# Attention with 192 queries and 1,024 keys: the third key load put behind a blank slot in one piece, and the output stores moved two pairs later

## The chip, the cores and the metric

The kernel runs on one core of one Trainium2 chip. The metric is the device time in microseconds (us). The profile is of one further execution; its span, from the first to the last instruction, was 812.8 us, in a run whose device time was 814.49 us.

## The reference

For 16 x 32 = 512 heads, with 192 queries, 1,024 keys and a head size of 128, all in bf16:

```python
B, H, Sq, Sk, D = 16, 32, 192, 1024, 128
...
scores = jnp.einsum("bhqd,bhkd->bhqk", q, k) * scale
p = _softmax(scores, axis=-1)
return jnp.einsum("bhqk,bhkd->bhqd", p, v)
```

## The kernel before

**Tiling.** Four heads make a *quad*; there are NQ = 128 quads, numbered x. The scores of one quad are made in three *fills* of PSUM, so there are NF = 384 fills, numbered f, and fill f belongs to quad f // 3. Each fill has a matching step of the second product, numbered s, which runs LAG = 4 fills later. TensorE's program is a plain alternation: `qk(f)` (L655, its matmuls at L670), then `pv(f - LAG)` (L678, matmuls at L699). One fill with its step takes about 2.05 us of TensorE, and one quad three times that. Ahead of fill 0 there is one blank fill (PRE = 1) and six blank steps (BLANK = 6) on cleared data, so that the loop's first round is like all others. The loop on TensorE (L715) holds six fills; what comes after it is straight code.

**The other engines.** VectorE transposes K (`turn_k`, L763, three pieces to a quad, three fills ahead) and Q (`turn_q`, L772), and normalises each finished step (`onorm`, L784 and L788) into the output buffer `f_ob`. GpSimd copies K into the order that TensorE reads (`order`, L620) and spreads V beside columns of ones (`spread`, L629). ScalarE takes the exponentials (L861, L864). There is one accumulator `f_o`, so `pv(s)` waits on `s_on` until `onorm(s - 1)` has read it. VectorE works strictly in its written order: while it waits for a K load, the `onorm` behind that transposition waits too, and TensorE with it.

**Loads.** K and V have five slots each (1 MB to a quad, 192 KB more for Q). All but one of the loads are issued by SyncE (SP) in one fixed order on one queue: each next V, then K, then Q, each held until its slot is free (`load_k` waits on `s_kx`, `load_v` on `s_pv`). At the start the order is written out by hand (L573 to L586). There, SP waits for two things: `s_qk >= PRE + 1` (fill 0 has been computed), and `s_pv >= BLANK - 2` (four of the blank steps are done). The load of quad 2's K stands around that second wait, in two halves of 512 KB.

**Stores.** The outputs of two quads (a *pair*) make one store of 384 KB; the last two quads are stored singly, the very last one in two halves. Slot i % NSO of `f_ob` holds store i. ScalarE issues store i after fill 6i + 12 + 6 * HOLD, which is seven pairs after the fills of that pair (`store_at`, L539). What would fall into the last 12 fills is left to SP, which issues it behind its last load (L596). With HOLD = 7 these are stores 54 to 64.

**The end.** After the last step VectorE checks the reciprocals, TensorE sums the two flags (L729, L730), all engines meet, each reads a flag that decides whether a general path has to be run (it isn't for this data), and SP waits in `stored` (L601) until every store has landed.

Of the kernel before, what the change touches and what calls it, by code (L numbers as in the profile page):

```python
# [421 lines left out]
def _attention_kernel(nc, q, k, v, out):  # L422
# [9 lines left out]
    NF = 3 * NQ  # L432
    LAG = 4

    PRE = 1
# [3 lines left out]
    NKN, NVS, NKT, NVP = 5, 5, 2, 2  # L439
    GQ = 2  # L440

    NSO, HOLD = 10, 7

    HELD = 2
    VB = 136
# [9 lines left out]
    with ExitStack() as outer:  # L455
        redo = outer.enter_context(nc.sbuf_tensor("redo", [1, 1], mybir.dt.int32))

        def sem(name):
            return outer.enter_context(nc.semaphore(name))
# [5 lines left out]
        s_kn = [sem("f_kn%d" % i) for i in range(NKN)]  # L465
# [7 lines left out]
        s_qk = sem("f_qk")  # L473
# [11 lines left out]
        with ExitStack() as es:  # L485
# [34 lines left out]
            def store(e, i):  # L520
                so = i % NSO
                x, c = stores[i]
                if x + c == NQ:

                    for y in range(2):
                        e.wait_ge(s_fin, y + 1)
                        e.dma_start(
                            of[4 * x + 2 * y:4 * x + 2 * y + 2].rearrange("x (p j) d -> (x p) (j d)", j=3),
                            ob[:, so, 3 * y:3 * y + 3, :].rearrange("p j d -> p (j d)"),
                        ).then_inc(s_st[so], 16)  # L530
                    return
                e.wait_ge(s_rc, 3 * (x + c) + 1)
                e.dma_start(
                    of[4 * x:4 * x + 4 * c].rearrange("(a x) (p j) d -> (x p) a (j d)", x=2, j=3),
                    ob[:, so, 0:6 * c, :].rearrange("p (a j) d -> p a (j d)", j=3),
                ).then_inc(s_st[so], 16)


            store_at = {3 * (x + c) + 6 + 6 * HOLD: i for i, (x, c) in enumerate(stores)  # L539
                        if 3 * (x + c) + 6 + 6 * HOLD <= NF - 12}  # L540

            def load_q(e, x):
                e.dma_start(
                    qn[:, x % NKN, :],
                    qf[4 * x:4 * x + 4].rearrange("a (j u) d -> (a j) (u d)", u=6).bitcast(U32),
                ).then_inc(s_qn[x % NKN], 16)
# [3 lines left out]
            def hint(eng):  # L550
                hints[eng.engine] = eng.mark_branch_hint_location()

            @block.sync
            def _(e):
                def load_k(x, lo=0, hi=32):
                    if x >= NKN:
                        e.wait_ge(s_kx, 3 * (x - NKN) + 3)
                    e.dma_start(
                        kn[:, x % NKN, 64 * lo:64 * hi],
                        kf[4 * x:4 * x + 4].rearrange("a (j r) d -> (a j) r d", r=32)[:, lo:hi, :]  # L560
                        .rearrange("p r d -> p (r d)").bitcast(U32),
                    ).then_inc(s_kn[x % NKN], 16)

                def load_v(x, lo=0, hi=4):
                    if x >= NVS:
                        e.wait_ge(s_pv, 3 * (x - NVS) + 2 + BLANK)
                    e.dma_start(
                        vs[:, x % NVS, lo:hi, :],
                        vf[4 * x + lo:4 * x + hi].rearrange("a (m t) d -> m a (t d)", t=T),
                    ).then_inc(s_v[x % NVS], 16)  # L570


                load_k(0)  # L573
                e.wait_ge(s_blank, 1)
                load_k(1)
                load_q(e, 1)
                load_v(0, 0, 2)
                e.wait_ge(s_qk, PRE + 1)
                load_v(0, 2, 4)
                load_k(2, 0, 16)  # L580
                e.wait_ge(s_pv, BLANK - 2)
                load_k(2, 16, 32)
                load_q(e, 2)
                for n in range(3, NKN):
                    load_v(n - 2)
                    load_k(n)  # L586
                    load_q(e, n)
                for n in range(NQ):
                    if n == NQ // 2:
                        hint(e)  # L590
                    if n + NKN - 2 < NQ:
                        load_v(n + NKN - 2)
                    if n + NKN < NQ:
                        load_k(n + NKN)
                        load_q(e, n + NKN)
                for i in range(len(store_at), len(stores)):  # L596
                    store(e, i)
            def stored(e):
                for so in range(NSO):
                    last = (len(stores) - 1) % NSO == so  # L600
                    e.wait_ge(s_st[so], 16 * (len(range(so, len(stores), NSO)) + last))  # L601
# [132 lines left out]
            def _(dve):  # L734
# [21 lines left out]
                def turn_k(g):  # L756
                    x, b = divmod(g, 3)
                    lo, hi = PIECES[b]
                    if b == 0:
                        dve.wait_ge(s_kn[x % NKN], 16 * (x // NKN + (2 if x % NKN == 2 else 1)))  # L760
                    if x >= 2:
                        dve.wait_ge(s_qk, 3 * (x - 2) + b + 1 + PRE)
                    dve.transpose(  # L763
                        kx[:, x % 2].rearrange("p (U s j u) -> p s u U j", s=2, j=32, u=2)[:, :, :, lo:hi],
                        kn[:, x % NKN].rearrange("p (s u U i) -> p s u U i", s=2, u=2, i=32)[:, :, :, lo:hi],
                    ).then_inc(s_kx, 1)
# [37 lines left out]
                def check(lo, hi, i, part):  # L804
# [9 lines left out]
                    dve.wait_ge(s_dv, cnt[0])  # L814

                turn_k(0)
                turn_q(0)
                for g in range(1, 5):
                    turn_k(g)
                turn_q(1)  # L820
                for f in range(NF + LAG + 1):
                    s = f - LAG - 1
                    if f == NF // 2:
                        hint(dve)
                    if s >= 0:
                        onorm(s)
                        if 0 <= s - EARLY < 3:
                            check(0, 2 * EARLY, 0, s - EARLY)
                    g = f + AHEAD
                    if 5 <= g < NF:  # L830
                        x, b = divmod(g, 3)
                        if b == 2 and x >= 2:
                            turn_q(x)
                        turn_k(g)
# [36 lines left out]
def bass_standalone__mha_softmax__near_ridge_kernel(  # L871
    nc: bass.Bass,
    q: bass.AP,
    k: bass.AP,
    v: bass.AP,
    out: bass.AP,
):
    _attention_kernel(nc, q, k, v, out)
# [28 lines left out]
```

## Time and profile before

| what | value |
|---|---|
| device time, three runs | median 814.06 us, 813.41 to 814.98 |
| span of the profiled execution | 812.8 us |
| TensorE matmul busy | 800.4 us, 98% |
| ScalarE busy | 749.9 us, 92% |
| VectorE busy | 599.3 us, 74% |
| GpSimd busy | 551.6 us, 68% |
| data moved | 319.20 MB, mean 393 GB/s |

A high share says that an engine had work nearly all the time, not that each of its instructions was on the path that sets the end. Of the 812.8 us TensorE was idle for 12.4 us in all; its idle stretches, and what they wait for, are what a change of loads and stores can touch. "Releaser" in a line's brackets is what ended the idle time before it; "issue" there means that the engine waited for nothing that the profile shows.

### The profile page before, as it was taken

How to read it: one execution, taken by the hardware profiler on the slowest of the kernel's cores; microseconds unless marked ns; L12 is line 12 of the kernel's file. 1: busy time of each engine (PE TensorE's matmuls, PEld its weight loads, DVE VectorE, ACT ScalarE, POOL GpSimd, SP SyncE). 2: the span in 40 equal slices, each digit the busy share in tenths (PEclk: the TensorE clock that was granted, in tenths of full speed). 3: DMA queues.
4: the chain of work that ended last, by engine and by line, in shares of the span. 5: the costliest groups of instructions: out<-in, count | busy, mean ns of one | idle time of the engine just before them, and what ended most of it. 6: DMA issues, size and time to landing. Idle time of an engine off the chain costs nothing. (4 is left out here: it accounts for less than half of the span.)

```text
span 812.8 us, 71452 instructions
## 1 busy us (share of the span) xinstructions
PE 800.4 (98%) x32996; PEld 714.3 (88%) x32996; DVE 599.3 (74%) x1293; ACT 749.9 (92%) x772; POOL 551.6 (68%) x648
## 2 busy tenths in 40 slices
PE   8999999999999999999999999999999999999996
PEld 6888888888888888888888888888888888888885
DVE  4777777777777777777777777777777777778773
ACT  6899999999999999999999999999999999999994
POOL 5676676676677667667667766766766776667762
PEclk9999999999999999999999999999999999999999
DMA  7999999999999999999999999999999999999995
GB/s 265 406 397 403 399 402 402 409 405 404 409 405 405 408 405 405 407 406 405 406 406 405 406 407 407 405 407 405 403 408 398 400 394 405 376 407 403 384 366 166
DMA packets 138474, 319.20 MB, mean 393 GB/s; under 512 B 7232, under 2 KB 56384, under 8 KB 122176
## 3 DMA queue, kind: packets, MB, share of 16 engines
q1 hardware_dynamic: 109776, 297.36, 93.7%
q10 hardware_dynamic: 28656, 21.43, 7.8%
q14 instruction: 35, 0.29, 0.1%
q8 instruction: 7, 0.11, 0.1%
HBM read 293.60 MB, written 25.17 MB: 392 GB/s over the span
## 5 line engine op out<-in xcount | busy, mean ns | idle before, releaser
L864 ACT ACTIVATE f_pt<-f_s 128x1536 bf16<-128x1536 f32 x384 | 554.9, 1445 | 0.0
L620 POOL COPY f_kt<-f_kx 128x768 uint32<-128x768 uint32 (+1 forms) x384 | 300.8, 787 | 212.4 <-DVE f_kx L763 212.3
L699 PE MATMUL f_o<-f_vp,f_pt 128*64 128x129 bf16 x12368 | 426.2, 222 | 1.6 <-PEq L653 1.4
L670 PE MATMUL f_s<-f_qt,f_kt 32*128 32x192 bf16 (+1 forms) x20528 | 422.8, 226 | 2.9 <-PEq L653 2.2
L699 PEld LDWEIGHTS f_o<-f_vp,f_pt 128*64 128x64 bf16 x12368 | 362.8, 110 | 50.6 <-issue 23.8
L670 PEld LDWEIGHTS f_s<-f_qt,f_kt 32*128 32x128 bf16 x20528 | 348.6, 92 | 39.4 <-issue 3.8
L763 DVE STREAM_TRANSPOSE f_kx<-f_kn 128x768 uint32<-128x768 uint32 (+1 forms) x384 | 333.8, 870 | 14.1 <-DMA f_kn<-in_k_dram 13.6
L629 POOL COPY f_vp<-f_vs 128x1024 uint32<-128x1024 uint32 x256 | 259.8, 1044 | 35.1 <-DMA f_vs<-in_v_dram 32.5
L861 ACT ACTIVATE f_pt<-f_s 128x512 bf16<-128x512 f32 x384 | 229.2, 597 | 51.5 <-PE f_s L670 8.1
L784 DVE RECIPROCAL f_rinv<-f_o 128x2 f32<-128x2 f32 x381 | 64.7, 170 | 178.2 <-PE f_o L699 178.1
L788 DVE TENSOR_TENSOR f_ob<-f_o,f_rinv 128x256 bf16<-128x256 f32 x381 | 161.6, 424 | 13.0
L772 DVE STREAM_TRANSPOSE f_qt<-f_qn 128x384 uint32<-128x384 uint32 x128 | 72.9, 570 | 0.0
L699 PE MATMUL f_s<-f_vp,f_pt 128*64 128x129 bf16 x96 | 3.3, 220 | 1.6 <-issue 1.5
L699 PEld LDWEIGHTS f_s<-f_vp,f_pt 128*64 128x64 bf16 x96 | 2.9, 110 | 1.9 <-issue 1.6
L848 ACT ACTIVATE f_pt<-f_ones 128x1536 f32<-128x1536 bf16 x3 | 4.2, 1472 | 0.0
L608 POOL MEMSET f_vp<- 128x1088 uint32 (+1 forms) x3 | 3.8, 1309 | 0.0
L848 ACT ACT_TABLE_LOAD x1 | 1.3, 1283 | 1.2 <-PEq L892 1.2
L784 DVE RECIPROCAL f_rinv<-f_s 128x2 f32<-128x2 f32 x3 | 0.5, 171 | 2.6 <-PE f_s L699 2.5
L712 PE MATMUL f_o<-f_ones 128*128 128x512 bf16 x2 | 1.0, 620 | 1.1 <-POOL f_ones L605 1.1
L736 DVE MEMSET f_pt<- 128x256 uint32 x4 | 1.1, 272 | 0.9 <-PEq L892 0.9
L729 PE MATMUL f_o<-f_bad,f_ones 128*1 128x1 bf16 x1 | 0.2, 165 | 1.4 <-DVEq L837 1.4
L788 DVE TENSOR_TENSOR f_ob<-f_s,f_rinv 128x256 bf16<-128x256 f32 x3 | 1.3, 425 | 0.3 <-DVE f_rinv L784 0.3
(15 smaller groups left out, 5.3 us busy)
## 6 DMA issues: line engine op xcount, KB each, us to landing
f_kn<-in_k_dram SPq DMA_DIRECT2D x127, 1024.0 KB, 18.0
f_vs<-in_v_dram SPq DMA_DIRECT2D x127, 1024.0 KB, 16.2
f_qn<-in_q_dram SPq DMA_DIRECT2D x127, 192.0 KB, 14.2
out_dram<-f_ob ACTq DMA_DIRECT2D x54, 384.0 KB, 9.6
out_dram<-f_ob SPq DMA_DIRECT2D x9, 384.0 KB, 7.2
f_vs<-in_v_dram SPq DMA_DIRECT2D x2, 512.0 KB, 6.1
f_kn<-in_k_dram SPq DMA_DIRECT2D x2, 512.0 KB, 5.6
f_qn<-in_q_dram ACTq DMA_DIRECT2D x1, 192.0 KB, 5.9
```

Of the source, the lines that this page charges most:

```text
L608: return gp.memset(part.bitcast(U32), 0x3F803F80)
L620: gp.tensor_copy(kt[:, x % NKT].bitcast(U32).rearrange("p U (j s u) c -> p U j s (u c)", s=2, u=2)[:, lo:hi], kx[:, x % 2].rearrange("p (U ...
L629: gp.tensor_copy(vp[:, x % NVP, 2 * T * i: 2 * T * i + 2 * T, 0:D].bitcast(U32), vs[:, x % NVS, 2 * i: 2 * i + 2, :].rearrange("p a (t d) ...
L670: ins = pe.matmul(S[:, c0: c0 + n1 - n0], kt[r, x % NKT, 2 * t + h, :, c], qt[r, x % R, h, n0:n1, c], start=w == 0 and g == 0, stop=w == 3 ...
L699: ins = pe.matmul(O[64 * z: 64 * z + 64, u, 0:129], pt[:, x % R, 2 * y + z, t * SQ + 64 * j: t * SQ + 64 * j + 64], vp[:, x % NVP, (2 * y ...
L763: dve.transpose(kx[:, x % 2].rearrange("p (U s j u) -> p s u U j", s=2, j=32, u=2)[:, :, :, lo:hi], kn[:, x % NKN].rearrange("p (s u U i) ...
L772: dve.transpose(qt[:, x % R].bitcast(U32).rearrange("p b (y j u) c -> p u y b (j c)", y=3, u=2), qn[:, x % NKN].rearrange("p (u y b i) -> ...
L784: dve.reciprocal(ri, O[:, :, 128]).then_inc(s_rc, 1)
L788: ins = dve.tensor_tensor(ob[:, so, 6 * a + 2 * w: 6 * a + 2 * w + 2, :], O[:, :, 0:128], ri.unsqueeze(2).to_broadcast([128, 2, D]), ALU.mult,
L848: return act.activation(part.bitcast(F32), ones[:, 0:1].to_broadcast([128, 2 * T * SQ // 2]), ACT_FN.Copy)
L861: act.activation(pt[:, x % R, 0, c], s1_ps[:], ACT_FN.Exp, scale=scale).then_inc(s_e1, 1)
L864: act.activation(pt[:, x % R, 1:4, c], s3_ps[f % 2][:], ACT_FN.Exp, scale=scale).then_inc(s_e3, 1)
```

## The change

Three things are changed. The output buffer has 12 slots in place of 10, and the stores that ScalarE issues come nine pairs behind in place of seven. Quad 2's K is loaded in one transfer of 1 MB, behind the wait for four blank steps; VectorE's wait for it counts one transfer in place of two. SP's stores behind the last load are now stores 52 to 64; the first four are issued as before, and ahead of the fifth (store 56) SP waits until the last score fill has been computed.

```diff
-    NSO, HOLD = 10, 7
+    NSO, HOLD = 12, 9
...
                 e.wait_ge(s_qk, PRE + 1)
                 load_v(0, 2, 4)
-                load_k(2, 0, 16)
                 e.wait_ge(s_pv, BLANK - 2)
-                load_k(2, 16, 32)
+                load_k(2)
                 load_q(e, 2)
...
                 for i in range(len(store_at), len(stores)):
+
+                    if i == len(store_at) + 4:
+                        e.wait_ge(s_qk, NF + PRE)
                     store(e, i)
...
                     if b == 0:
-                        dve.wait_ge(s_kn[x % NKN], 16 * (x // NKN + (2 if x % NKN == 2 else 1)))
+                        dve.wait_ge(s_kn[x % NKN], 16 * (x // NKN + 1))
```

## The prediction, made before the changed kernel was run

> **What bounds the kernel now.** I read the page first: TensorE is at 98%, and the DMA engines are as full.
>
> ```profile
> span 812.8 us, 71452 instructions
> ...
> PE   8999999999999999999999999999999999999996
> ...
> DMA  7999999999999999999999999999999999999995
> GB/s 265 406 397 403 399 402 402 409 405 404 409 405 405 408 405 405 407 406 405 406 406 405 406 407 407 405 407 405 403 408 398 400 394 405 376 407 403 384 366 166
> ```
>
> So TensorE sets the pace and the transfers only just keep up. A fill with its step takes 2.053 us (1.03 for each half in the chain of waits), 384 of them 788.4. That time the change cannot touch; it can touch the 12.4 us in which TensorE is idle. The next view is TensorE's order of time at the start:
>
> ```profile
> 8.67 1.10 PE L670 MATMUL f_s<-f_qt,f_kt 32*128 32x192 bf16 x48 [1.78 <-PEq L653]
> ...
> 17.84 0.34 PE L670 MATMUL f_s<-f_qt,f_kt 32*128 32x128 bf16 x9 [0.51 <-issue]
> ...
> 27.84 1.10 PE L699 MATMUL f_o<-f_vp,f_pt 128*64 128x129 bf16 x32 [1.39 <-PEq L653]
> ```
>
> After fill 0 (8.67) TensorE loses 0.51 and 1.39 us. VectorE's order of time says where the 1.39 comes from:
>
> ```profile
> 19.75 1.84 DVE L763 STREAM_TRANSPOSE f_kx<-f_kn 128x768 uint32<-128x768 uint32 x2 [6.65 <-DMA f_kn<-in_k_dram]
> ...
> 26.11 0.98 DVE L763 STREAM_TRANSPOSE f_kx<-f_kn 128x768 uint32<-128x768 uint32 x1 [2.09 <-DMA f_kn<-in_k_dram]
> 27.02 0.13 DVE L784 RECIPROCAL f_rinv<-f_o 128x2 f32<-128x2 f32 x1
> 27.18 0.42 DVE L788 TENSOR_TENSOR f_ob<-f_o,f_rinv 128x256 bf16<-128x256 f32 x1
> ```
>
> At 19.75 it begins on K2, which landed at 19.73; at 26.11 on K3, which landed at 26.09. The normalisation of step 2 stands behind that transposition and ends at 27.60; step 3 on TensorE waits for it. Until quad 6 each K is taken within 0.7 us of its landing: the start is bound by how much has been loaded. For the late part I read the waits from 690 to 790 us:
>
> ```profile
> POOL f_vp L629 <- DMA f_vs<-in_v_dram: 23.2, 15, 2.2
> ...
> DVE f_kx L763 <- DMA f_kn<-in_k_dram: 0.5, 2, 0.3
> PE f_s L670 <- PEq L653: 0.4, 1, 0.4
> ```
>
> The loads have fallen behind: comparing landings with transpositions in the trace, a K lies ready 6.9 us ahead at quad 21, and 0.02 us ahead at quad 117. The fall begins with the first store (124.87 us). One of the 16 landings of each load is late by then, by some 5 us: one DMA engine lags. TensorE loses 0.12 + 0.45 = 0.57 us at 745 to 748. Last, the end, in order of time:
>
> ```profile
> 778.69 27.40 SPq L533 DMA_DIRECT2D out_dram<-f_ob  x10
> ...
> 804.42 1.97 PE L699 MATMUL f_s<-f_vp,f_pt 128*64 128x129 bf16 x63 [1.46 <-issue]
> ...
> 807.09 1.25 SPq L527 DMA_DIRECT2D out_dram<-f_ob  x2
> ```
>
> The 1.46 us is a wait for instructions. The trace's DMA packets show one of 16,384 bytes at 802.14, 0.95 us long; TensorE goes on 1.33 us after its end. The 0.51 us at 17.33 is the same thing: packet at 15.55, 0.96 us long, TensorE on 1.33 us later. Counting back 256 instructions from each stall gives the moments at which the block before was entered: 13.98 and 799.04. From there to the packet took 1.57 us at the start, but 3.10 us at the end, where stores fill all DMA engines (315 to 328 GB/s in each us from 797 to 802).
>
> **What the Trainium skill says.** "Runtime: NRT & Kernel Launch", section "Instruction fetch mechanics": instructions are refilled in blocks of 16 KiB, 256 instructions, over a DMA queue of the sequencer's own. The packet size and the count back agree. "DMA: Bandwidth & Descriptors", section "Queues, rings and completion order": each DMA engine goes round the queues that have work, a packet of several descriptors at a time. That fits 1.53 us more on full engines. The same page, "Issuing engines are not separate DMA queues": transfers from all engines share 16 DMA engines; hence a store delays loads whichever engine issues it. Here the slack falls from the first store on.
>
> **The change part by part.** The sum is made against the span of 812.8; its run took 814.49, at the upper side of 813.41 to 814.98, so I carry the difference to the median, 814.06.
>
> *K2 in one piece.* Removed: 512 KB of load issued at 10.22, which moved from 12.7 to 15.5, and one DMA issue. Added: nothing; the half is moved past the wait that ends at 14.4. So DMA engines are idle from about 13 to 15.2, where before they moved about 0.5 MB. At 400 GB/s that is worth 1.3 us, if the rest runs as before: K2, Q2, V1, K3 all land 1.3 later, and as the start is bound by loads, TensorE with them. Against it: before, 15 to 18.5 ran at 123 to 265 GB/s, with packets of 4,096 bytes taking up to 1.04 us in place of 0.16. If K2's 128 packets of 8,192 bytes run near their usual 0.31 us, eight to an engine, K2 is through at 15.2 + 2.5 + about 0.9 for slow first ones (K0's took 0.4 to 1.0) = 18.6; its second half ended at about 18.3. Then nearly all comes back. Range -0.3 to +1.3; I take +0.4. The fetch at 15.55 meets emptier engines, but a gain there is swallowed by the wait for K3: 0. VectorE's changed count costs 0. Issued later on SP behind K2: Q2, V1, K3, all counted in this. SP's issue of one transfer (0.34 to 1.9 us) lies beside data still moving.
>
> *Nine pairs.* ScalarE issues 52 stores in place of 54 (0.38 us each on its queue, beside its 92%, hidden by TensorE), from 149.5 us on in place of 124.87. At any later time two stores fewer lie ahead of the loads, and the lagging engine needs 1.04 us for its part of one (the spacing of its landings, 796.80 to 803.12). So 1.5 to 2.1 us more slack, more than the 0.57 lost: -0.57 to 0, I take -0.5. The slot for store i is freed by store i - 12 at the same distance of 11 fills as i - 10 before: 0. The two buffers need memory, not time.
>
> *The last stores.* Stores 52 to 55 go out as 54 to 57 did; all their data landed at 798.3 but for the lagging engine (799.9, or 2 us earlier by the slack). So the block asked for at 799.04 meets free engines: packet at 800.6, TensorE ready at 802.9, where it needs it at 802.96. Of 1.46 us all is gained on TensorE, VectorE's check and the meeting of engines. But seven stores now start at 800.7 (end of the last fill). Queued behind SP's new wait are stores 56 to 64 and SP's part in `stored`. No slot waits on these: quads 126 and 127 need stores 51 and 52. Their 4,096 packets (7 x 512 and 512 for the last two quads) go at about 410 a microsecond (the count from 797 to 802): 10.0 us from 801.5, so the last lands at about 811.9. Before, SP found all landed at 811.1, and the span ended at 812.76 because ScalarE's last instruction came at 812.46, 1.9 us after its branch, behind instruction packets of 0.45 to 1.34 us. With SP's exit of 0.6 after 811.9 the end is 812.5; ScalarE's fetch, 1.5 us longer among stores but begun 1.46 earlier, gives about the same. So -0.3; bounds -1.46 (stores faster) and +1.9 (below).
>
> Sum: +0.4 - 0.5 - 0.3 = -0.4 us; 814.06 - 0.4 gives **813.6 us**. Within 0.2% is 1.63 us either way, about what a measurement can tell.
>
> **Rivals.** *Faster:* K2 at its usual packet rate costs -0.3, the late waits go (-0.57), and the lagging engine's rate (1.04 us a store) holds for all, so the stores end 1.5 us earlier and TensorE's 1.46 counts in full: -2.3, 811.7 us. For it: the medians of packets elsewhere. Against it: from 797 to 802 full engines took 1.23 us a store. *Slower:* the stores behind the last fill become the end. If they run at 389 packets a microsecond (the rate at 793) they need 10.5 us, and if the engine that lags also carries the instruction blocks (0.95 + 1.33 us seen at 802 and 805), its last landing is near 813.9 and the span ends at 814.6: +1.8, 815.9 us. It decides from the point where the last landing passes 812.1. *Only the start counts:* K2's missing half costs its 1.3 in full, the rest cancels: 814.9, still inside 0.2%. That the change does not do what it says is excluded for the stores: SP reached store 56 at 790, so the new wait does hold.
>
> **How the numbers follow.** Likeliest: the terms cancel within 0.2%, 0.47 (with the third rival), own range 812.5 to 815.0. Faster by more: 0.33, which also takes in executions that lose more at 745 than this one did (the runs differ by 1.6 us). Slower: 0.20. The range 811.4 to 815.9 reaches to both outer rivals and leaves about 2 in 10 out.
>
> **What would show it.** K2 landing at 19.5 to 20.5, K3 at 26 to 27 and a wait of 1.2 to 2.4 us before step 3; no idle TensorE at 745 to 748 and fewer waits of GpSimd for V; no 1.46 before the step after the last fill; the last landing 0.5 to 1 us later than the meeting of engines. I am wrong if K3 lands before 25, if TensorE's stall at the end stays, or if the last landing is past 813.

## The result, and the profile after

The changed kernel took 818.15 us (median of 4 runs, 816.39 to 818.69) against 814.11 us of the kernel before (4 runs): a ratio of 1.0045, with a 95% interval of 1.0027 to 1.0063. It is slower, by 4.0 us. Among the experiments the same kernel was measured again, 22 runs against 51: 816.16 us against 814.36, ratio 1.0017 (1.0004 to 1.0029). So 1.8 us of the slowdown came back, and the other 2.2 us of the first measurement need an explanation of their own.

The profiled execution of the changed kernel fell among the longer ones (its run took 818.18 us). Its page:

```profile
span 816.4 us, 71451 instructions
...
PE   8899999999999999999999999999999999999995
...
GB/s 261 399 397 402 399 401 402 402 404 409 407 403 410 405 404 410 406 405 408 406 404 409 405 405 408 403 405 403 397 404 405 389 403 397 398 408 402 374 318 162
```

The body of the run looks the same. The span is 3.6 us longer, and three moments of TensorE's order of time divide it:

| stretch | before | after | difference |
|---|---|---|---|
| start of the span to the start of fill 30 | 74.04 | 75.84 | +1.80 |
| fill 30 to the start of the last fill (383) | 725.54 | 726.02 | +0.48 |
| start of the last fill to the end of the span | 13.18 | 14.58 | +1.40 |

**The start.** The order of time of TensorE and VectorE, to be held against the lines of before:

```profile
26.40 0.98 DVE L765 STREAM_TRANSPOSE f_kx<-f_kn 128x768 uint32<-128x768 uint32 x1 [2.77 <-DMA f_kn<-in_k_dram]
...
28.13 1.36 PE L701 MATMUL f_o<-f_vp,f_pt 128*64 128x129 bf16 x32 [2.08 <-PEq L655]
29.42 1.89 PE L672 MATMUL f_s<-f_qt,f_kt 32*128 32x128 bf16 x48
```

K3 landed at 26.38, 0.29 later than before, and TensorE waited 2.08 us for it in place of 1.39. The wait of 0.51 us for a block of instructions (the *fetch stall*) at 17.8 no longer shows as a wait: the block's packet began at 15.00 in place of 15.55, and the fill at 16.24 took 1.28 us in place of 1.10, so about 0.2 us of it is left. But the fill at 29.42 then takes 1.89 us where its like took 1.09: TensorE runs at half its clock. The table by stretches has the granted clock as its last column but two. First before, then after:

```profile
27.00:34.00 7.00, 6.16 (x256) 5.54 (x256) 5.68 (x14) 5.30 (x6) 5.12 (x6) 1.00 1.04 406
```

```profile
27.00:34.00 7.00, 5.87 (x168) 5.15 (x170) 4.64 (x11) 3.11 (x4) 4.27 (x5) 0.76 1.05 413
```

The clock records of the trace show it as one window of 3.41 us at 0.5, from 28.82. From step 3 (28.13) to the second fill behind it (32.72) TensorE takes 4.59 us, where the same three pieces took 3.08 before: 1.5 us are lost. With the 0.29 us by which K3 came later, this is the whole +1.80 of the start. The window just ahead of it (25.41 to 28.82) holds the whole wait of 2.08 us. Both kernels have one such window at fill 0 already (from 9.94 before, from 8.34 after).

**The body.** GpSimd's waits for V fell from 32.5 to 5.6 us, and a K lies ready 3.6 us ahead of its use at quad 114 (0.7 before). Half of that slack has nothing to do with stores: at quad 8, long before the first store, it is 2.8 us in place of 1.5, about the 1.5 us by which the window of half clock held TensorE back while the loads went on. TensorE gained nothing by it. Its idle time near 745 us even grew, which is most of the +0.48 of the body; in the waits from 690 to 790 us:

```profile
PE f_s L672 <- PEq L655: 0.7, 1, 0.7
PE f_o L701 <- PEq L655: 0.2, 1, 0.2
```

VectorE's order of time at that point shows what else is there, the early check of the reciprocals:

```profile
745.89 1.07 DVE L809 TENSOR_SCALAR f_chk<-f_rinv 128x702 f32<-128x702 f32 x1
748.59 1.01 DVE L811 TENSOR_TENSOR f_chk<-f_chk,f_rinv 128x702 f32<-128x702 f32 x1
751.05 0.88 DVE L813 TENSOR_REDUCE f_bad<-f_chk 128x1 bf16<-128x702 f32 x1
```

These stand between the transpositions that TensorE waits for. The first took 1.07 us here; before, it took 0.52:

```profile
744.09 0.52 DVE L807 TENSOR_SCALAR f_chk<-f_rinv 128x702 f32<-128x702 f32 x1
```

That the idle time is the check's is tested below.

**The end**, in order of time:

```profile
780.97 29.95 SPq L533 DMA_DIRECT2D out_dram<-f_ob  x12
...
805.66 1.97 PE L701 MATMUL f_s<-f_vp,f_pt 128*64 128x129 bf16 x63 [0.42 <-issue]
...
810.97 1.88 SPq L527 DMA_DIRECT2D out_dram<-f_ob  x2
```

TensorE's stall for its block of instructions fell from 1.46 to 0.42 us (the packet began at 802.78 on free DMA engines, but took 1.39 us in place of 0.95), and VectorE finished 7.4 us after the last fill in place of 8.4. But SP's last issue ended at 812.85, so SP came to the meeting of all engines at 813.02, 2.7 us after VectorE's last operation; before, SP was there ahead of VectorE. The trace's issues show why: SP's first issue behind the last fill takes 0.37 us, its last three of a pair take 1.15 to 1.33 us, and each of these ends when 15 or 16 of the 16 landings of the store three places ahead of it are in. The last store landed at 814.87, 11.9 us after the last fill, and SP left at 815.31. The span was ended by ScalarE, whose last instruction came at 816.14, 1.9 us after its branch behind the meeting. So here the late meeting set the end; the landing alone would have ended the span near 815.5 (an estimate from SP's 815.31 and the 0.2 us that came behind SP in the last experiment).

### The profile page after: what moved, and what is told of

Its sections match the earlier page's. It is cut to its first block, busy times and chain, and to the rows that moved or that the text cites. A ratio compares the mean times of both kernels' runs of the same rounds, so it can differ in the third digit from the quotient of the medians.

```text
span 816.4 us, 71451 instructions
## 1 busy us (share of the span) xinstructions
PE 801.1 (98%) x32996; PEld 715.0 (88%) x32996; DVE 599.2 (73%) x1293; ACT 750.0 (92%) x772; POOL 551.6 (68%) x648
```

## The experiments

My theory after this result: the end costs 1.2 to 1.4 us in every execution; the start costs up to 1.8 us, mostly by a window of half clock; the body costs nothing. The rival: one of the two edits carries the whole 4 us. Each kernel below was timed beside the kernel before, in four groups on four chips (the kernel before took 814.25, 814.36, 814.07 and 814.01 us in them), and profiled once. A ratio is not the quotient of the two medians beside it, and can differ from it by 0.001.

**K2 alone.**

```diff
-                load_k(2, 0, 16)
                 e.wait_ge(s_pv, BLANK - 2)
-                load_k(2, 16, 32)
+                load_k(2)
```

VectorE's wait again counts one transfer.

> Only quad 2's K is loaded whole behind the wait for four blank steps; the stores are as before. My theory: the start alone costs 1.8 us, of which some 0.7 are a longer wait for K3 before step 3 and some 1.2 to 1.6 a second window of half TensorE clock that this wait brings about: 815.9 us where the window is there, 814.4 to 814.8 in executions without it. Rival: the start costs at most the 0.3 us by which K3 landed later, the rest of the 4 us is in the stores: 814.4 us in all executions.

Measured: 813.37 against 814.25 us, ratio 0.9986 (0.9976 to 0.9997). Neither: it did not cost anything. It was run a second time, beside other starts:

> Quad 2's K whole behind the wait for four blank steps, alone, a second time beside the other starts. So far it measured -0.9 us, while four of five profiles with this start were about 1.5 to 2 us longer there than those with K2 in halves. If the start does cost that, 815 to 816 us here; if the first measurement holds, 813.4 us; if the start only varies, within 0.5 us of the kernel before.

Measured: 814.24 against 814.07, ratio 1.0002 (0.9987 to 1.0017). The profile of this second run, though, has the start of the changed kernel nearly exactly: a wait of 2.10 us ahead of step 3 and a window of half clock from 28.96. The first had a wait of 1.80 and no window there:

```profile
28.06 1.10 PE L698 MATMUL f_o<-f_vp,f_pt 128*64 128x129 bf16 x32 [1.80 <-PEq L652]
```

So the long start occurs with K2 whole, but an average over executions doesn't show a cost, and my theory that this edit costs 1.8 us at the start falls.

**The stores alone.**

```diff
-    NSO, HOLD = 10, 7
+    NSO, HOLD = 12, 9
...
+                    if i == len(store_at) + 4:
+                        e.wait_ge(s_qk, NF + PRE)
                     store(e, i)
```

> Twelve slots, nine pairs, and the wait ahead of the fifth of SP's stores; K2 is loaded in halves as before. My theory: the end alone costs 1.2 to 1.4 us, because SP reaches the meeting of engines some 2 us late: 815.4 us; TensorE's stall after the last fill falls from 1.46 to about 0.4 us. Rival: the stores carry nearly all of the change, through contention in the body of the run: 817.5 to 818 us.

Measured: 815.75 against 814.25, ratio 1.0024 (1.0012 to 1.0035). From the last fill's start to the end it took 14.5 us, TensorE's stall was 0.36. The slowdown that comes back is here. The start of this execution, with K2 in halves, had a fetch stall of 1.62 us:

```profile
17.61 0.34 PE L672 MATMUL f_s<-f_qt,f_kt 32*128 32x128 bf16 x9 [1.62 <-issue]
```

**Nine pairs without the wait** (the first two lines of that diff alone).

> Twelve slots and nine pairs, without the wait for the last score fill; K2 in halves. My theory: loads land 1.5 to 3 us further ahead of their use at 700 us, GpSimd's waits for V fall from 32 us to under 10, and the time stays within 0.5 us of before, since TensorE did not wait for loads after the start: 814.1 us. Rival, as I predicted: the loss of TensorE near 745 us goes with it, 813.5 us.

Measured: 813.41 against 814.25, ratio 0.9992 (0.9978 to 1.0006); the end took 13.15 us, the stall 1.52. The later stores don't cost. The slack that I expected did not come: GpSimd waited 39.8 us for V, more than before, and a K lay ready 0.14 us ahead of its use at quad 114. The time alone would fit the rival (813.5 us) as well, but TensorE still idled at 745 and 751, by 0.52 us.

**Five behind** (the stores alone, with `len(store_at) + 6`).

> As the stores alone, but the wait stands ahead of the seventh of SP's stores, so that five stores and the last two quads' parts come behind the last fill in place of seven. My theory: SP's queue takes about three stores before it holds SP up, so SP gets through its issues about when VectorE is done, the stall of TensorE is still cut by about 1 us, and the end is 1 us earlier than before: 813.1 us. Rivals: SP is still late at the meeting, 814.5 us or more; or the stores ahead of the wait still delay the instruction block, 814.1 us.

Measured: 813.82 against 814.25, ratio 1.0002 (0.9989 to 1.0015). In the profile the end took 11.9 us, 1.3 less than before: TensorE has no fetch stall at all, and SP is through 0.7 us after VectorE's last operation.

```profile
803.17 3.27 PE L701 MATMUL f_s<-f_vp,f_pt 128*64 128x129 bf16 x96
```

All 96 matmuls of the three steps ahead of the last one go through in one piece; the packet took 0.96 us here. The gain of the end is seen in the profile; the timed runs don't resolve it.

**The changed kernel again.**

> The changed kernel as it is, on the chip and in the rounds of the other experiments. If its parts add up (K2 alone measured -0.9 us, the stores alone +1.5), it takes 814.7 to 815.5 us, and the 818.15 of the first measurement holds some 3 us of a start that varies from execution to execution (with one or two windows of half clock). Rival: the parts work on each other (a late K3 always brings the second window of half clock), and it is 817 to 818.5 us again.

Measured: 816.16 against 814.36 (22 and 51 runs), ratio 1.0017 (1.0004 to 1.0029). Nearer to the sum of the parts than to the first measurement. The runs lie from 815.18 to 818.89; the four that are over 818 have a mean clock of 0.993 or 0.994, the eight below 816 of 0.997 or 0.998. The first measurement had 0.994, 0.992, 0.994 and 0.996, the last of them in its shortest run. The profile of the second measurement is one of the long runs (818.14 us) and has two windows of half clock by fill 30 as well, but by another wait: K2 landed at 21.27, not at 19.34, and the window follows TensorE's wait for it.

```profile
23.80 1.94 PE L700 MATMUL f_o<-f_vp,f_pt 128*64 128x129 bf16 x32 [2.13 <-PEq L654]
```

**K2 and five behind; three behind** (both edits, with `+ 6` and `+ 8`).

> K2 whole, nine pairs, and the wait ahead of SP's seventh store: five stores and the last quads' parts behind the last fill. If the costs are as the parts showed, the end is 1.3 us shorter than in the kernel before (11.9 from the last fill's start to the end of the span, in place of 13.2), the start as with K2 alone: 812.5 to 813 us, faster than before. Rival: the start of this version takes the 1.8 us that the profile of the changed kernel showed: 814.5 to 815 us.

> As the run before, with the wait ahead of SP's ninth store: three stores and the last quads' parts behind the last fill. SP isn't held up then and comes to the meeting before VectorE, but stores 58 and 59 are still under way when TensorE asks for its last block: the stall is 0.7 to 1.5 us. 813 to 813.5 us. If the number of stores behind the wait didn't matter, it would be as with seven, some 815 us.

Measured: 814.04 (ratio 0.9991, 0.9977 to 1.0005) and 813.94 (0.9998, 0.9985 to 1.0012), against 814.36. The ends took 11.8 and 12.1 us. The times are 0.4 to 1.5 us above those expected, and with three behind the expected stall of 0.7 to 1.5 us did not come: TensorE went on without one. Both profiles had long starts, with fill 30 at 75.74 and 77.00. In the first of them the wait ahead of step 3 was longer than in the changed kernel, but no window of half clock followed it; both of its windows lie at fill 0.

```profile
29.54 1.10 PE L700 MATMUL f_o<-f_vp,f_pt 128*64 128x129 bf16 x32 [2.33 <-PEq L654]
```

**The check 30 steps earlier.**

```diff
-    EARLY = NF - 33
+    EARLY = NF - 63
```

> The kernel before, with VectorE's early check of the reciprocals 30 steps earlier (and the late check over 60 columns more). If the idle time of TensorE near 745 us is this check's, which holds VectorE for 2.4 to 3 us in three steps, it moves to about 684 us and stays 0.5 to 1 us. If it is the loads', as I predicted, it stays at 745. The time is within 0.3 us of before either way.

Measured: 814.76 against 814.36, ratio 1.0007 (0.9991 to 1.0022). VectorE and TensorE in order of time:

```profile
683.65 1.17 DVE L809 TENSOR_TENSOR f_chk<-f_chk,f_rinv 128x642 f32<-128x642 f32 x1
...
685.85 1.10 PE L670 MATMUL f_s<-f_qt,f_kt 32*128 32x64 bf16 x64 [0.62 <-PEq L653]
```

The idle time moved with the check: 0.10 and 0.62 us at 683 and 686, and none at 745. This execution had the shortest start of all (fill 30 at 72.19) and its K loads lay ready only 0.02 us ahead of their use from quad 90 on; TensorE lost 0.56 us at 617 and five times 0.08 to 0.30 from 748 on. So a short start can leave the loads late, and TensorE waits for them. The loads can cost something late in the run, but that isn't what the profile before showed.

**K2 whole behind fill 0, and no wait for blank steps.**

```diff
-                load_k(2, 0, 16)
+                load_k(2)
                 e.wait_ge(s_pv, BLANK - 2)
-                load_k(2, 16, 32)
```

VectorE's wait counts one transfer; the second kernel leaves out the line with `e.wait_ge` too.

> Quad 2's K whole, but ahead of the wait for four blank steps, just behind the second half of the first V; the rest as in the kernel before. If the start is bound by what has been loaded, all of 1 MB moves where DMA engines were partly idle, K3 lands 1 to 1.5 us earlier, and TensorE's wait ahead of step 3 falls under 0.8 us; the block of instructions asked for at about 14 us may come later, which costs up to 1.5 us there. Sum -0.5 us, 813.8 us. If the wait for K3 is not set by the amount loaded, it stays at 1.4 us.

> SP's wait for four blank steps is left out, so K2 whole, Q2, V1, K3 and all behind them go out in a row behind fill 0. K3 should land at about 23.5 us in place of 26, so that step 3 does not wait for it; in exchange TensorE's wait for its block of instructions near 17.5 us grows to about 1.6 us, as at the end of the program. Sum -0.3 to -1 us, 813.6 us. Rival: a longer wait for instructions brings a second window of half clock, 815.5 us.

Measured: 812.89 (ratio 0.9982, 0.9971 to 0.9993) and 816.09 (1.0016, 1.0003 to 1.0028), against 814.07. TensorE's order of time, first with the wait, then without:

```profile
18.38 0.34 PE L669 MATMUL f_s<-f_qt,f_kt 32*128 32x128 bf16 x9 [1.39 <-issue]
```

```profile
21.21 0.34 PE L668 MATMUL f_s<-f_qt,f_kt 32*128 32x128 bf16 x9 [4.13 <-issue]
```

These two waits are for the same block of instructions, 0.51 us in the profile before. The 1.39 us shows nothing by itself: with K2 in halves this stall lay between 0.25 and 1.62 us in six profiles. The 4.13 us lies outside that; the packet began 5.15 us after the block before it was entered, in place of 1.57. In the first kernel, K3 landed at 24.95 and step 3 didn't wait; that trade came out ahead. In the second, K3 landed no earlier (25.02), and the wait brought a second window of half clock. That the wait for four blank steps keeps the way open for the instructions fits the 4.13 us, but isn't shown: a later kernel that has it stalled by 2.99 us.

**Seven pairs, five behind** (the wait alone, ahead of store 58).

> The kernel before, with ten slots and seven pairs, and only the wait added, ahead of SP's fifth store (store 58), so that five stores and the last quads' parts come behind the last fill. If the end depends on the number behind the wait and not on the pairs, the last fill's start to the end of the span takes 11.8 to 12 us, as with nine pairs, and the time is 813.3 us. If the pairs matter, it is 814.3 us or more.

Measured: 814.15 against 814.07, ratio 0.999 (0.9974 to 1.0005); the end took 11.9 us. The number of stores behind the wait sets the end, not the pairs. The time is not the 813.3 us expected: the profile had one of the longest starts (fill 30 at 77.16, two windows of half clock), with K2 in halves.

**Both better parts together** (K2 whole behind fill 0, nine pairs, five behind).

> The two parts that came out well in one kernel: K2 whole ahead of the wait for four blank steps, and twelve slots, nine pairs, with five stores and the last quads' parts behind the last fill. If they add up, the start is that of the first alone (-1.2 us) and the end 11.9 us in place of 12.6 to 13.2 from the last fill's start: 812.0 to 812.5 us. If they do not, 813 us.

Measured: 814.47 against 814.01, ratio 1.0005 (0.999 to 1.0021). The end took 11.9 us, but the wait for instructions near 18 us was 2.99 in this profile, against 1.39 with the same order of loads, and brought a window of half clock from 20.27. They do not add up to a faster kernel; that K2 whole behind fill 0 is a gain rests on one measurement.

**The last four from ScalarE** (against the changed kernel).

```diff
-                    store(e, i)
+                    if not len(store_at) + 7 <= i < len(stores) - 2:
+                        store(e, i)
...
                     if f in store_at:
                         store(act, store_at[f])
+                for i in range(len(store_at) + 7, len(stores) - 2):
+                    store(act, i)
```

> The changed kernel, but of the seven stores behind the last fill SP issues only three; the other four (59 to 62) are issued by ScalarE on its own queue, behind its last exponential; the last quads' parts stay with SP. The bytes behind the last fill are the same. If the end is long because SP comes late to the meeting, SP is through before VectorE now, the meeting comes 1.5 to 2 us earlier, and from the last fill's start to the end of the span it takes 13.6 to 13.9 us in place of 14.6; the rest is the time that the data take. 815.2 us. If the data alone set the end, it stays at 14.6 us and 816.2 us.

Measured: 816.54 against 814.01, ratio 1.0021 (1.0007 to 1.0035). SP's waits in this kernel from 800 us on:

```profile
SPq L533 <- PE f_s L673: 9.5, 1, 9.5
SPq L604 <- DMA out_dram<-f_ob: 3.1, 1, 3.1
```

SP was through at 808.21, 7.8 us after the last fill (10.1 in the changed kernel), and the meeting came that much earlier. The end still took 14.66 us: now SP waits 3.1 us in `stored` (L604) for a store to land. So an earlier meeting alone brought nothing here. But the data were not the same chain as before either: the last store landed 12.9 us after the last fill, 1.0 us later than in the changed kernel; why stays open. In the changed kernel two chains end within a microsecond of each other, SP's issues with the meeting behind them, and the landing of the data; this run takes away the first and lengthens the second.

The starts and ends of all profiles, from the trace (us):

| kernel | fill 30 begins | windows of half clock by then | last fill to end |
|---|---|---|---|
| before | 74.04 | 1 | 13.18 |
| changed; again | 75.84; 75.64 | 2; 2 | 14.58; 14.74 |
| K2 alone; again | 74.27; 75.90 | 1; 2 | 12.33; 12.16 |
| stores alone (seven behind) | 73.18 | 0 | 14.50 |
| nine pairs, no wait | 73.64 | 1 | 13.15 |
| five behind | 75.21 | 1 | 11.86 |
| K2 and five; and three behind | 75.74; 77.00 | 2; 2 | 11.79; 12.10 |
| check earlier | 72.19 | 0 | 12.45 |
| K2 behind fill 0; no blank wait | 73.10; 77.41 | 1; 2 | 12.63; 12.36 |
| seven pairs, five behind | 77.16 | 2 | 11.91 |
| both better parts | 75.10 | 1 | 11.90 |
| last four from ScalarE | 73.31 | 0 | 14.66 |

With the wait, the end goes by the number of stores behind it: 14.5 to 14.7 for seven, 11.8 to 11.9 for five, 12.1 for three. Without it, it lies between 12.2 and 13.2; the two longest have the two longest fetch stalls there (1.46 and 1.52 us), the others 0.15 to 0.70 us. The start varies by 5 us, in no clear order by kernel. In 198 runs of the kernel before, those with a mean clock of 0.999 or more had a median of 813.33 us (54 runs), those at 0.996 or less 815.80 us (51 runs).

## Why the prediction was wrong, point by point

**The step that failed is "the last stores", put at -0.3 us: it cost +1.40 in the profile**, and some 1.5 us in the timed runs of the stores alone. Of its parts, the instruction block was right in kind: TensorE needed 1.04 us less (0.42 in place of 1.46), where I said all of 1.46. The landing was near: 11.9 us after the last fill, where I reckoned 11.2 (811.9 less 800.7). What I had wrong is the path. I set the landing against the span's end as it was, took 0.6 us for SP's exit, and put SP's issues at nothing, as lying beside the data. But by the issue times SP gets only some three stores ahead of the landings, so its issues last nearly as long as the data, SP came to the meeting 2.7 us after VectorE, and all that stands behind the meeting (3.2 us before, 3.4 here) began later. The landing alone would have cost some 0.5 us (815.5, against the end of before moved with the last fill, 815.0; an estimate). The rival "slower" had the stores behind the last fill as the new end, and the last landing did pass its point; but it named the landing, not SP's issues and the meeting. That its +1.8 us is what the second measurement gave is luck in the number. I gave it 2 in 10.

**K2 in one piece (+0.4, from -0.3 to +1.3).** K2 landed at 19.34, 0.39 us earlier than before and just ahead of the 19.5 to 20.5 that I gave; K3 landed 0.29 us later, in its range. That the gain in the fetch at 17.8 would be swallowed: right. The second window of half clock, 1.5 us, was put at nothing: I forecast a wait of 1.2 to 2.4 us ahead of step 3, and the trace before showed a window of half clock behind the wait of 1.78 us ahead of fill 0, but I had no term for what the wait does to the clock. By the mean clocks of the timed runs it is likely what makes the first measurement longer than the second; timed runs have no trace, so this isn't shown. Alone, K2 whole measured -0.9 and +0.2 us; it isn't shown to cost anything.

**Nine pairs (-0.5).** The slack rose by about 2.9 us at quad 114, where 1.5 to 2.1 were forecast, but 1.4 us of that were there at quad 8, ahead of any store. That nine pairs give slack isn't shown: nine pairs without the wait had 0.14 us at quad 114, and K2 alone, the second time, had 3.06 with seven. And the slack gave no time: I had taken TensorE's 0.57 us at 745 for a wait for loads, since one late K stood beside it. It is VectorE's check, as the run that moved it shows. That GpSimd waited less for V (5.6 us) did not help TensorE either. In the profile before the slack stops growing soon after the first store, at 136 us, but falls only from 179 us on.

**Slips in the working.** The rival "only the start counts" comes to 815.4 us, not 814.9, if the rest cancels; it is still inside 0.2%. The stores' 10.0 us from 801.5 end at 811.5; the 0.4 us to 811.9 has no source. The 798.3 us is the landing of store 58; that of store 57 was 796.7. None of these changes which term failed.

What stays open: how often the long start occurs with each order of loads. Profiles show two windows in five of seven starts with K2 whole behind the blank steps (three behind the wait for K3, one behind a wait for K2, one with both at fill 0, ahead of K2's load) and in one of six with K2 in halves, yet the timed runs of K2 alone have no cost. Whether the 2.2 us, over half of the slowdown, that the first measurement adds was chance alone wasn't settled either. Nor was how far the end would fall if SP came early to the meeting and the data landed no later.

## What to carry to other kernels

Work that is moved behind the last compute has to be counted as a queue of its own: how long the issuing engine is held up, when it comes to the point where all engines meet, and when the last byte lands; here six stores' worth (five pairs and the last two quads) fitted behind the last fill and eight didn't. A gap in the bounding engine need not belong to the wait that stands nearest to it: move the suspect and see whether the gap moves. Where executions differ by more than the effect, look at which stretch of the program differs, and compare that stretch.

## What the runs showed of the hardware that was not expected

- Half clock came in windows of 3.41 us, and by what TensorE had idled in the window before, not by the length of a wait. From 1.97 to 2.59 us of idle time inside one window halved the next (2.08 us in the changed kernel). A wait of 2.33 us that fell into two windows, 1.25 and 1.08 us (K2 and five behind), did not. Around 1.8 us it went both ways: 1.78 us at fill 0 did it (before), 1.80 us ahead of step 3 did not (K2 alone, first run). One window at fill 0 was halved behind 0.80 us of idle time in a window that was itself at half clock (K2 and five behind). The windows are counted in steps of 3.41 us from those on record. The halved window of the changed kernel behind step 3 cost 1.5 us.
- A block of 16,384 bytes of TensorE's instructions took about 3.9 us from the moment its predecessor was entered until TensorE could go on (1.57 to the packet, 0.96, 1.33), more than the 3.4 us in which TensorE used up 256 instructions there (13.98 to 17.33). The stall at this place varied from execution to execution: 0.25 to 1.62 us with K2 in halves, 1.39 and 2.99 us in two kernels with the same order of loads at the start. In the stalls of 1.39, 2.99 and 4.13 us the packet itself took 0.96 to 0.98 us; it began 2.33, 3.99 and 5.15 us after the block before it was entered.
- With stores alone on the DMA engines, 377 to 434 packets of 768 bytes were started in a microsecond: 290 to 333 GB/s (changed kernel, each microsecond from 804 to 813), where the body of the run moved about 405.
